# A decode block on one core: wq in five row loads, with the load of x between them on SyncE's queue

## The chip, the cores and the metric

The kernel runs on one core of one Trainium2 chip. The metric is device time in microseconds (us) for one execution.

## What is computed

One decode step of a transformer block for one token: a layernorm, attention over a long cache with 32 query heads and 4 key/value heads, a residual, a second layernorm and a gated feed-forward layer. Cut to what matters:

```python
# x (1,1,1024); k_cache, v_cache (1,4,65536,128); wq (1024,4096); wo (4096,1024)
# w_gate, w_up (1024,3584); w_down (3584,1024); all bfloat16
q = layernorm(x) @ wq                       # 32 heads of 128
p = softmax(q . k_cache * 128 ** -0.5)      # 8 heads share one k/v head
h = x + (p @ v_cache) @ wo
n = layernorm(h)
out = h + (gelu(n @ w_gate) * (n @ w_up)) @ w_down
```

Everything but x is read once: 8 MiB of wq, 64 MiB of keys, 64 MiB of values, 8 MiB of wo and three times 7 MiB of the feed-forward weights, 165 MiB (173.02 MB) in all.

## The kernel before, in words

**The ring.** All large tensors pass through one tile, `ring` (L86): 128 partitions, three slots of 64 KB per partition, so 8 MiB a slot. The helper `load` (L171 to L179) takes the next slot and issues one DMA on SyncE's queue. Each such DMA covers all 128 partitions, with one contiguous piece of DRAM per partition: 64 KB in a load of wq, keys, values or wo, 56 KB in one of w_gate or w_up.

**The order of the loads** on SyncE's queue is wq, then pieces of 8 MiB of keys and values in the order of `todo` (L389 to L392), then wo, w_gate, w_up, and w_down in five pieces of falling size (L591 to L611). A load waits, at its issue, until the work that read its slot's earlier content is done. The first three loads have three free slots; the fourth (the third of keys) needs wq's slot and so waits for the matmuls with wq.

**The start.** The function `first_load_leads` (L119) takes the first instruction of SyncE, the load of wq, out of the body of the program and puts it ahead of the barrier that all engines pass at the start. The load of x, 2 KB, into four rows (0, 32, 64, 96) of the tile `x_row` goes onto ScalarE's queue (L183) after VectorE has set `x_row` to zero (L182). Then:

- GpSimd and VectorE build constants (L187 to L203): the identities, `sel`, `hmask`, `esel`; GpSimd clears `wsel` (L198).
- When x has landed, VectorE transposes it (L230) and `layernorm_cols` (L207 to L226) runs a chain over VectorE, TensorE and GpSimd. Its result is put into the padded tile `xnz` (L234 to L238, L250).
- When wq has landed, 64 small matmuls (L254 to L257) form q in PSUM; VectorE transposes it (L260) and casts it (L261); four matmuls spread it over the partitions (L264), and ScalarE writes it into `wsel` (L268), the stationary operand of all score matmuls.
- The first key load is then transposed in place on VectorE (L287), scored on TensorE (L289 to L299), and so on through the key and value heads. TensorE's, VectorE's and ScalarE's orders in that part are written out by hand (`keep`, L134; the loop at L409).

The lines that matter here:

```python
wq_v = A_wq.rearrange("(p c) n -> p c n", c=DC)
nc.vector.memset(x_row[:], 0.0)
nc.scalar.dma_start(out=x_row[0:97:32, :], in_=A_x[0, 0].rearrange("(g n) -> g n", g=4))
assert DC * HD == 2 * CW
wq_t = load(wq_v[:])
```

Row p of the tile thus holds rows 8p to 8p+7 of wq, 64 KB that lie together in DRAM.

Of the kernel before, what the change touches and what calls it, by code (L numbers as in the profile page):

```python
# [17 lines left out]
def kernel(  # L18
# [13 lines left out]
    nc = tc.nc  # L32
    P = 128
    D = A_x.shape[-1]
    Hkv, Sk, Dh = A_k_cache.shape[1], A_k_cache.shape[2], A_k_cache.shape[3]
    HD = A_wq.shape[1]
# [10 lines left out]
    CW = 16384  # L47
# [29 lines left out]
    x_row = lead.tile([P, D // 4], BF16, name="x_row")  # L77
# [8 lines left out]
    ring = chpool.tile([P, NSLOT * 2 * CW], BF16, name="ring")  # L86
# [81 lines left out]
    slot = [NSLOT - 1]  # L168
    loads, pools, last = [], [], {}

    def load(src, off=0):  # L171
        n, w = src.shape[1], src.shape[2]
        if off == 0:
            slot[0] = (slot[0] + 1) % NSLOT
        assert off + n * w <= 2 * CW
        o = slot[0] * 2 * CW + off
        tv = ring[:, o:o + n * w].rearrange("p (n w) -> p n w", w=w)
        loads.append(nc.sync.dma_start(out=tv, in_=src).ins)
        return tv  # L179

    wq_v = A_wq.rearrange("(p c) n -> p c n", c=DC)
    nc.vector.memset(x_row[:], 0.0)  # L182
    nc.scalar.dma_start(out=x_row[0:97:32, :], in_=A_x[0, 0].rearrange("(g n) -> g n", g=4))  # L183
    assert DC * HD == 2 * CW
    wq_t = load(wq_v[:])

    make_identity(nc, ident_bf[:])  # L187
    make_identity(nc, ident_f[:])
# [11 lines left out]
    for bp in range(4):  # L200
        s0 = 64 * (bp // 2) + bp % 2
        nc.vector.tensor_copy(out=esel[:, bp, :, :],
                              in_=ident_bf[:, s0:s0 + 63:2].unsqueeze(1).to_broadcast([P, 4, 32]))  # L203
# [205 lines left out]
    for n, u in enumerate(units):  # L409
        what, g, li = u  # L410
# [237 lines left out]
```

## Time and profile before

| what | value |
|---|---|
| time, median of 3 runs | 407.19 us (407.12 to 407.48) |
| time of the profiled execution | 407.47 us |
| its span, first to last instruction | 405.7 us |
| read from HBM | 173.02 MB |
| busy: TensorE matmul, VectorE, ScalarE, GpSimd | 295.1, 204.1, 40.3, 7.5 us |
| DMA, mean over the span | 427 GB/s |
| issue to landing of an 8 MiB load of keys, of values (medians) | 38.4, 34.2 us |
| last matmuls that wait for a load start at | 401.7 us |

The profiled execution's own time is 0.07% above the median, and 1.8 us longer than its span; that is what lies around the span. The profile page lists busy times by engine, the span in 40 slices, the DMA queues, the chain of work that ended last, and the groups of instructions. The timeline lists instructions in order of time, with the start, the length, the engine, the line and the tiles; "<-" in brackets names what ended the wait before. SPq and ACTq are the queues of SyncE and ScalarE, where DMAs are issued; PEld is TensorE's loading of stationary operands.

### The profile page before, as it was taken

To read this page: it belongs to the slowest core of one execution; us is meant where nothing else is said; L and a number is where in the kernel's file an instruction comes from. 1 tells how busy PE (TensorE), PEld (TensorE's weight loads), DVE (VectorE), ACT (ScalarE), POOL (GpSimd) and SP (SyncE) were. 2 spreads that over 40 slices of the span, in tenths; PEclk is the share of its full clock that TensorE was granted. 3 is DMA by queue.
4 is the path that set the end of the run, shared out by engine and by line. 5 is a ranking of instruction groups with operands and counts; after the bars stand their busy time and mean duration, and the time that the engine had idled before them with its cause. 6 is when DMAs were issued, how large, how long until landed. Compare 5 with 4: busy or idle time off the path is not lost.

```text
span 405.7 us, 2613 instructions
## 1 busy us (share of the span) xinstructions
PE 295.1 (73%) x1519; PEld 59.5 (15%) x681; DVE 204.1 (50%) x187; ACT 40.3 (10%) x63; POOL 7.5 (2%) x17
## 2 busy tenths in 40 slices
PE   0150777657799696979969957997796899655286
PEld 0110111111111110131111103111110211211012
DVE  0210978999829743972596387609943100220211
ACT  1010000013000021100000312000022100100001
POOL 2000000000000000000000000000010000000000
PEclk9995589999899999769999968899899699886779
DMA  9999999999999999999999999999999999999996
GB/s 414 414 414 465 465 414 409 420 414 491 426 415 426 414 485 426 415 426 420 485 420 415 433 420 478 420 416 439 420 465 426 415 446 420 439 443 419 424 409 249
DMA packets 3629, 173.18 MB, mean 427 GB/s; under 512 B 414, under 2 KB 674, under 8 KB 802
## 3 DMA queue, kind: packets, MB, share of 16 engines
q1 hardware_dynamic: 3610, 173.02, 98.8%
q8 instruction: 8, 0.13, 0.1%
q14 instruction: 3, 0.02, 0.0%
q10 hardware_dynamic: 8, 0.00, 0.0%
HBM read 173.02 MB, written 0.00 MB: 426 GB/s over the span
## 4 chain that ended last, share of the span: by engine, by line
DMA 40%; PE 37%; DVE 19%; ACT 2%; issue 1%; ACTq 0%; DVEq 0%
DMA ring<-in_A_k_cache_dram 30%; PE acc_ps L157 16%; DVE ring L287 14%; DMA ring<-in_B_w_down_dram 11%; PE qk_ps L155 7%; PE qk_ps L157 6%; PE acc_ps L155 5%; DVE mx L312 2%; ACT sc L308 2%; DVE pT L345 1%; PE o_ps L155 1%; DVE acc_sb L368 1%; PE at_ps L155 1%; PE at_ps L157 0%; PE nb_ps L155 0%
## 5 line engine op out<-in xcount | busy, mean ns | idle before, releaser
L287 DVE STREAM_TRANSPOSE ring<-ring 128x2048 uint32<-128x2048 uint32 x64 | 142.5, 2279 | 37.4 <-DMA ring<-in_A_k_cache_dram 37.4
L155 PE MATMUL qk_ps<-ring,wsel 128*128 128x512 bf16 x256 | 107.7, 421 | 51.5 <-DVE ring L287 32.0
L157 PE MATMUL qk_ps<-ring,wsel 128*128 128x512 bf16 x256 | 107.1, 418 | 0.0
L157 PE MATMUL acc_ps<-ring,pT 128*128 128x512 bf16 x384 | 105.2, 383 | 0.0
L155 PEld LDWEIGHTS <-wsel 128*128 128x128 bf16 x256 | 27.2, 106 | 158.8 <-issue 143.2
L155 PE MATMUL acc_ps<-ring,pT 128*128 128x512 bf16 x128 | 49.2, 385 | 0.0
L312 DVE TENSOR_REDUCE mx<-qk_ps 128x1 f32<-128x1024 f32 x16 | 19.5, 1220 | 25.8 <-ACT sc L308 19.7
L345 DVE STREAM_TRANSPOSE pT<-pT 128x1024 bf16<-128x1024 bf16 x16 | 19.3, 1228 | 23.8 <-ACT pT L339 23.8
L308 ACT COPY sc<-qk_ps 128x1024 f32<-128x1024 f32 x12 | 12.1, 1012 | 151.0 <-PE qk_ps L157 151.0
L155 PEld LDWEIGHTS <-pT 128*128 128x128 bf16 x128 | 12.8, 100 | 90.8 <-issue 90.8
L368 DVE COPY acc_sb<-acc_ps 32x512 f32<-32x512 f32 x8 | 5.3, 666 | 29.5 <-PE acc_ps L157 29.5
L339 ACT ACTIVATE pT<-sc,nbias 128x1024 bf16<-128x1024 f32 x12 | 13.7, 1142 | 45.0 <-DVE nbias L331 42.1
L155 PE MATMUL wu_ps<-ring,hnz 128*32 128x448 bf16 x32 | 5.9, 738 | 8.8 <-DMA ring<-in_B_w_up_dram 8.8
L155 PE MATMUL ln_tot<-ln_s,ones_f 128*128 128x1 f32 x8 | 1.9, 311 | 13.5 <-DVE ln_s L209 11.7
L155 PE MATMUL wg_ps<-ring,hnz 128*32 128x448 bf16 x32 | 6.1, 737 | 6.8 <-DMA ring<-in_B_w_gate_dram 6.8
L155 PE MATMUL o_ps<-sel,acc_sb 128*128 128x8 f32 x32 | 6.6, 335 | 5.8 <-DVE rl L382 5.4
L155 PE MATMUL q_ps<-ring,xnz 128*32 128x512 bf16 x32 | 4.2, 502 | 9.0 <-DMA ring<-in_A_wq_dram 9.0
L370 ACT COPY acc_sb<-acc_ps 32x512 f32<-32x512 f32 x8 | 4.6, 578 | 58.7 <-DVE acc_sb L368 58.7
L511 DVE STREAM_TRANSPOSE wu_t<-wu_ps 128x448 f32<-128x448 f32 x2 | 1.2, 628 | 14.2 <-PE wu_ps L155 14.2
L511 DVE STREAM_TRANSPOSE wg_t<-wg_ps 128x448 f32<-128x448 f32 x2 | 1.2, 629 | 13.3 <-PE wg_ps L155 13.3
L260 DVE STREAM_TRANSPOSE q_t<-q_ps 128x512 f32<-128x512 f32 x2 | 1.3, 695 | 12.5 <-PE q_ps L157 12.5
L339 ACT ACTIVATE pT<-qk_ps,nbias 128x1024 bf16<-128x1024 f32 x4 | 4.5, 1114 | 29.8 <-PE acc_ps L157 16.8
(117 smaller groups left out, 98.5 us busy)
## 6 DMA issues: line engine op xcount, KB each, us to landing
ring<-in_B_w_gate_dram SPq DMA_DIRECT2D x1, 7168.0 KB, 35.2
ring<-in_B_w_up_dram SPq DMA_DIRECT2D x1, 7168.0 KB, 38.3
ring<-in_B_w_down_dram SPq DMA_DIRECT2D x1, 4096.0 KB, 39.2
ring<-in_B_w_down_dram SPq DMA_DIRECT2D x1, 2048.0 KB, 43.2
ring<-in_B_w_down_dram SPq DMA_DIRECT2D x1, 768.0 KB, 44.6
ring<-in_B_w_down_dram SPq DMA_DIRECT2D x2, 128.0 KB, 44.5
ring<-in_A_k_cache_dram SPq DMA_DIRECT2D x8, 38.4
ring<-in_A_v_cache_dram SPq DMA_DIRECT2D x8, 34.2
```

The costliest lines, as they stand in the source:

```text
L155: return pe(t.matmul(out, lhsT=lhsT, rhs=rhs, start=start, stop=stop, tile_position=tile_position, skip_group_check=skip_group_check))
L157: op = t.add_instruction(mybir.InstMatmult(name=nc.get_next_instruction_name(), engine=t.engine, start_tensor_calc=start, stop_tensor_calc ...
L260: nc.vector.transpose(out=q_t[:, k, :], in_=q_banks[k])
L287: dv(nc.vector.transpose(out=kt[:, c * w:(c + 1) * w], in_=kt[:, c * w:(c + 1) * w]))
L308: ac(nc.scalar.copy(out=sc[:], in_=flat))
L312: dv(nc.vector.tensor_reduce(out=state[("mx", g)][:, li:li + 1], in_=flat, axis=AX.X, op=ALU.max))
L339: ac(nc.scalar.activation(out=flat, in_=state.pop(("sc", g, li)), func=ACT.Exp, bias=st["nbias"][:, 0:1], scale=scale, accum_out=st["lpart ...
L345: dv(nc.vector.transpose(out=flat, in_=flat))
L368: dv(nc.vector.tensor_copy(out=acc_sb[sl, :], in_=acc[sl, c, :]))
L370: ac(nc.scalar.copy(out=acc_sb[sl, :], in_=acc[sl, c, :]))
L511: nc.vector.transpose(out=t[:, k, :], in_=banks[k][:, 0:HF * 32])
```

## The change

wq is no longer one load of 128 rows but five, of 16, 16, 32, 32 and 32 rows, all on SyncE's queue and into the same slot. The load of x moves from ScalarE's queue to SyncE's, between the second and the third of them. `first_load_leads` is unchanged and now takes the load of the first 16 rows ahead of the barrier.

```diff
 wq_v = A_wq.rearrange("(p c) n -> p c n", c=DC)
 nc.vector.memset(x_row[:], 0.0)
-nc.scalar.dma_start(out=x_row[0:97:32, :], in_=A_x[0, 0].rearrange("(g n) -> g n", g=4))
 assert DC * HD == 2 * CW
-wq_t = load(wq_v[:])
+slot[0] = 0
+wq_t = ring[:, 0:2 * CW].rearrange("p (n w) -> p n w", w=HD)
+
+def wq_rows(lo, hi):
+    loads.append(nc.sync.dma_start(out=wq_t[lo:hi], in_=wq_v[lo:hi]).ins)
+
+wq_rows(0, 16)
+wq_rows(16, 32)
+nc.sync.dma_start(out=x_row[0:97:32, :], in_=A_x[0, 0].rearrange("(g n) -> g n", g=4))
+for lo in range(32, P, 32):
+    wq_rows(lo, lo + 32)
```

The order of instructions changes with it in three places. On SyncE's queue stand: wq rows 0 to 15, the barrier, wq rows 16 to 31, x (which waits for the memset of `x_row`), the three loads of 32 rows, and then the keys as before. On VectorE the eight operations for `esel`, `sel` and `hmask` now stand ahead of the transpose of x; on GpSimd the memset of `xnz` stands ahead of the layernorm's power. On TensorE the order is the same; the first weight load from `xnz` and the first matmul with wq wait for the five loads where they waited for one.

## The prediction

> **What bounds the kernel now.** I read the page's slices first, then the issues of DMAs, then the timeline of the start and the chain of work that ended last. The slices and the sum of what was read:
>
> ```profile
> DMA  9999999999999999999999999999999999999996
> ...
> HBM read 173.02 MB, written 0.00 MB: 426 GB/s over the span
> ```
>
> The DMA row shows nine tenths or more in every slice but the last, while no engine comes near that over the span. From the timeline of the start, which names what each wait ended on:
>
> ```profile
> 0.00 0.38 SPq L178 DMA_DIRECT2D ring<-in_A_wq_dram  x1
> 9.75 0.62 DVE L230 STREAM_TRANSPOSE x_t<-x_row 128x256 bf16<-128x256 bf16 x1 [8.56 <-DMA x_row<-in_A_x_dram]
> 14.55 0.10 PEld L155 LDWEIGHTS <-xnz 128*32 128x32 bf16 x1 [1.72 <-DVE xnz L237]
> 21.89 0.62 PE L155 MATMUL q_ps<-ring,xnz 128*32 128x512 bf16 x4 [8.97 <-DMA ring<-in_A_wq_dram]
> 28.98 1.06 ACT L268 CAST wsel<-qr_ps 32x128 bf16<-32x128 f32 x4 [25.30 <-PE qr_ps L155]
> 41.17 11.09 DVE L287 STREAM_TRANSPOSE ring<-ring 128x2048 uint32<-128x2048 uint32 x5 [12.59 <-DMA ring<-in_A_k_cache_dram]
> ```
>
> wq is there at 21.89, the first keys at 41.17: 19.28 us for the next 8 MiB (8.389 MB), or 435 GB/s. Everything else in the start has room: xnz is ready at 14.55, 7.3 us before wq; wsel is done at 30.04, 11.1 us before the keys. The chain of work that ended last, farther on:
>
> ```profile
> 158.36 39.15 DMA ring<-in_A_k_cache_dram
> 197.53 8.90 DVE ring L287 x4
> ...
> 233.65 41.05 DMA ring<-in_A_k_cache_dram
> 274.73 8.90 DVE ring L287 x4
> ...
> 357.32 43.21 DMA ring<-in_B_w_down_dram
> ```
>
> Keys are there at 197.51 and at 274.70; between the two, four 8 MiB loads landed: 77.19 / 4 = 19.30 us each, the same pace. And a load takes about 39 us from issue to landing where 19.3 are its own: each is issued while the one ahead of it still has its whole time to go, so the stream never runs dry. It closes as a sum: 165 MiB at 19.29 us per 8 MiB is 397.9 us, plus 2.6 us (21.89 - 19.29) until the first load is at pace, is 400.5; the page's chain ends its last DMA at 357.32 + 43.21 = 400.53. The rest, to 405.7, is the tail behind the last rows of w_down. So **the one stream of loads sets the end**, and what an edit costs it anywhere is paid in full.
>
> **What the change removes.** One issue on ScalarE's queue (1.08 us, started at 1.07). Behind it there stood a table load that ended at 3.46, and ScalarE's next work is at 28.98: nothing gained.
>
> **What it moves.** x, on SyncE, waits for the memset of x_row, which ended at 1.04 (0.87 + 0.17). Behind it stand three loads of wq and then the keys, each an issue of 0.33 to 0.38 us, as the rows of SPq show. The last wq load is then issued by about 2.6 us and the keys by 3.3, instead of 0.78. What hides it: 2 MiB of wq are queued ahead of x, at least 2 x 2.41 = 4.8 us of stream from about 1.0 on, so to 5.8 us. Without that cover the stream would lose 0.35 us for each issue. x now lands behind 2 MiB: at some 7 us at today's pace, or after two loads at whatever pace they have. The chain from x to xnz took 14.55 - 9.75 = 4.8 us; the eight operations now ahead of it on VectorE (busy from 13.03 to 14.10 before) and the 0.31 us memset on GpSimd need only the identities (1.70 us) and run before x is there. xnz must be ready when wq is. Cost and gain: 0 as long as x lands 4.8 us before wq. The third key load waits for five semaphores of wq in place of one, but also, as before, for the matmuls with wq, which come later: 0.
>
> **What it adds: five loads with few rows each.** This is the disputed cost, and no row shows it: every large load of the trace spreads over 128 rows, its 16 DMA engines together at 435 GB/s (27.2 GB/s each). A load of 16 rows has 16 packets of 64 KB, one for each engine if they spread; but these engines all write into 16 neighbouring rows. *Lower end:* the engine is the limit and not the place it writes to. Then 8 MiB take 19.3 us in whatever pieces, and the cost is 0. *Upper end:* the rate goes with the rows. A row then takes 435 / 128 = 3.4 GB/s, 16 rows take 54 GB/s, and each of the five loads, whatever its height, lasts as long as a full one: 5 x 19.3 = 96.5 us, +77.2. In between, think of the store as having doors, each as fast as an engine, and ask how many of the 16 a load reaches. If 16 rows reach 2 doors (eight neighbouring rows to a door) and 32 rows 4, that is the upper end; with 4 and 8 doors each load lasts 4 x 2.41 = 9.65 us, 48.2 us for wq, +28.9; with 8 and 16 doors 4.83 each, 24.1 for wq, +4.8; with 16, nothing. What in the trace speaks for a limit on the store's side: the pace of 19.3 us is the same for wq, keys and values, early and late, under busy and idle engines, so it is a fixed one, and is reached with all rows in play. What speaks against it: engine and door would have to be equally fast. Of the four cases three cost. I take the value nearest the middle of the ends: the geometric mean of 19.3 and 96.5 is 43.2 us, and the case nearest to it is 4 and 8 doors, **48.2 us, +28.9**.
>
> [...]
>
> **The sum.** wq is there 28.9 us later, at 50.8. The keys follow in the queue at the old pace, and what lies between (8.15 us from wq to wsel, inside 19.28) shifts with both. No later place gives the time back, since the stream has no idle time to give. The profiled execution: 407.47 + 28.9 = 436.4; against the median, which lies 0.28 us lower, 407.19 + 28.9 = **436.1 us**. Own range of this case: 432 (some engines run ahead of others into the next load, and part of the waiting overlaps) to 442 (each of the four further loads also pays the 1.5 us that the first one takes beyond 19.3 us from its first packet at about 1.0).
>
> **The rivals.**
> - *Partial cost:* 8 and 16 doors, or doors shared so unevenly that the loads overlap: +4.8 to +24, 412 to 431 us. For it: queues of 16 engines need not march in step. Against: equal packets on equal engines, which now start within a us of each other (983 GB/s of packets start between 1.0 and 2.0 us, which is 15 of 64 KB).
> - *Rows are the limit:* +77.2, 484 us. Against: it takes the coarsest doors.
> - *The change does nothing,* because the rate belongs to the engine: 407.2 us, within 0.2%. For it: 27.2 GB/s on each of 16 engines, for any tensor.
> - *Faster, on the other side:* the place is the start of the stream. The first load needs 21.89 - 19.28 = 2.6 us beyond its pace, of which 1.0 us passes before nearly all first packets. The price is the 1.5 us left; if a load of 16 rows is set up sooner than one of 128, the most of it could go, say 1.1: 406.1 us. It decides only if 16-row loads run at the full 435 GB/s: already a pace 6% lower (1.1 of 19.3 us) on wq would eat it.
>
> **How the numbers follow.** Cases: +28.9 with its own range 0.70; partial cost 0.09; rows 0.05; nothing 0.09; faster 0.07. The bound of 0.2% (0.8 us) is about what a measurement of this kernel can tell from no change. Slower: 0.70 + 0.09 + 0.05 = 0.84; same 0.09; faster 0.07. The first two cases hold 0.79, so the range reaches down to the case of no change, the lower end of the unknown cost, at 406.4 (407.2 - 0.8), and holds 0.88; the upper end at 484 stays out. The likeliest case's own range is 432 to 442.
>
> **What would show it.** In the changed profile: the first matmul with wq at 50 to 52 us, not 21.89; the first key transpose 19.3 us behind it; in the slices of the first 48 us about 175 GB/s on average (8.39 MB in 48 us), first near 109, if a load of 1 MiB takes as long as one of 2; x transposed at about 21 us; later distances between landings still 19.3 us; all engines idle longer before their first keys. I am wrong if the first matmul with wq stays near 22 us, and partly wrong (the size of the doors) if it lies near 27 or 99. If wq lands late but the end does not move by as much, then the stream had idle time that I did not see.

## The result and the profile after

The changed kernel takes 436.68 us (median of 5 runs, 436.66 to 436.83) where the kernel before takes 407.48 (median of 5, 407.12 to 407.73): a ratio of 1.0721, 95% interval 1.0709 to 1.0733. It is 29.2 us slower. The span of its profiled execution (436.68 us) is 434.9 us, 29.2 more than before. The ratios below leave out runs that a slower state of the core disturbed; for the one kernel whose median that would shift, the profiled run is given instead.

The slices of the page after; the rows are the busy share of the DMA engines in tenths and the bytes moved:

```profile
DMA  9599999999999999999999999999999999999996
GB/s 193 97 193 193 289 398 470 398 466 404 465 404 464 405 458 410 458 410 454 416 452 416 448 422 446 422 446 423 440 429 446 428 436 434 426 418 454 431 405 262
...
HBM read 173.02 MB, written 0.00 MB: 398 GB/s over the span
```

The bytes are the same, and the engines are as busy as before in nearly all slices; but in the first four slices (43 us) they move less than half as much as later. A packet is counted whole in the slice in which it starts, so the 5 and the 97 of the second slice are no pause: most of that slice is filled by packets that started in the first. The engines are busy but not fast here: their packets last longer. The windows show how much longer. The first load of 16 rows is 16 packets of 64 KB, counted where they start, with the time that they took as a share of 16 engines over the window, here 1.0 to 3.0 us, of the changed kernel:

```profile
q1 hardware_dynamic: 16, 1.05, 427.5%
```

and the same window of the kernel before:

```profile
q1 hardware_dynamic: 15, 0.98, 145.5%
```

4.275 x 16 x 2.0 / 16 = 8.6 us for a packet, against 1.455 x 16 x 2.0 / 15 = 3.1. All 16 packets of the changed kernel start between 1.0 and 2.0 us, so all 16 engines work on the load of 16 rows at once; it is not that fewer engines serve a load of few rows. The timeline after, in the order of the lines shown of before:

```profile
0.00 1.11 SPq L188 DMA_DIRECT2D ring<-in_A_wq_dram  x2
...
1.87 1.39 SPq L188 DMA_DIRECT2D ring<-in_A_wq_dram  x3
...
3.30 54.25 SPq L178 DMA_DIRECT2D ring<-in_A_k_cache_dram  x3
...
21.00 0.63 DVE L239 STREAM_TRANSPOSE x_t<-x_row 128x256 bf16<-128x256 bf16 x1 [16.43 <-DMA x_row<-in_A_x_dram]
25.31 0.18 DVE L246 COPY xnz<-xn_bf 128x8 bf16<-128x8 bf16 x1
...
51.84 0.62 PE L155 MATMUL q_ps<-ring,xnz 128*32 128x512 bf16 x4 [27.67 <-DMA ring<-in_A_wq_dram]
...
59.16 1.06 ACT L277 CAST wsel<-qr_ps 32x128 bf16<-32x128 f32 x4 [56.87 <-PE qr_ps L155]
...
70.94 11.09 DVE L296 STREAM_TRANSPOSE ring<-ring 128x2048 uint32<-128x2048 uint32 x5 [12.17 <-DMA ring<-in_A_k_cache_dram]
```

wq is there at 51.84, 29.95 us later; the keys follow it by 19.10 us (19.28 before), so their pace is the old one; wsel is ready at 60.22, 10.7 us ahead of them. Farther on, the chain of work that ended last:

```profile
262.96 41.14 DMA ring<-in_A_k_cache_dram
304.12 8.90 DVE ring L296 x4
```

The same keys are there at 304.10, 29.40 later than at 274.70 before. So what wq lost at the start is carried to the end, nearly in full.

### The profile page after: what moved, and what is told of

The parts are those of the page before. It is cut to its first block, busy times and chain, and to the rows that moved or that the text cites. A ratio compares the mean times of both kernels' runs of the same rounds, so it can differ in the third digit from the quotient of the medians.

```text
span 434.9 us, 2618 instructions
## 1 busy us (share of the span) xinstructions
PE 297.6 (68%) x1516; PEld 59.3 (14%) x681; DVE 206.3 (47%) x187; ACT 40.3 (9%) x63; POOL 7.5 (2%) x17
## 4 chain that ended last, share of the span: by engine, by line
PE 47%; DMA 29%; DVE 17%; another core or an unknown queue 3%; ACT 2%; issue 1%; SPq 0%; ACTq 0%; DVEq 0%
PE acc_ps L157 17%; DVE ring L296 12%; DMA ring<-in_A_wq_dram 11%; DMA ring<-in_A_k_cache_dram 9%; PE qk_ps L155 9%; PE qk_ps L157 9%; DMA ring<-in_B_w_up_dram 9%; PE acc_ps L155 6%; DVE mx L321 2%; ACT sc L317 2%; DVE pT L354 2%; PE wu_ps L155 1%; PE wu_ps L157 1%; PE o_ps L155 1%
## 5 line engine op out<-in xcount | busy, mean ns | idle before, releaser
L155 PE MATMUL qk_ps<-ring,wsel 128*128 128x512 bf16 x256 | 108.7, 425 | 49.9 <-DVE ring L296 30.2
L157 PE MATMUL qk_ps<-ring,wsel 128*128 128x512 bf16 x256 | 108.3, 423 | 0.0
L155 PE MATMUL acc_ps<-ring,pT 128*128 128x512 bf16 x128 | 49.2, 385 | 0.0
```

Of the source, the lines that this page charges most:

```text
L155: return pe(t.matmul(out, lhsT=lhsT, rhs=rhs, start=start, stop=stop, tile_position=tile_position, skip_group_check=skip_group_check))
L157: op = t.add_instruction(mybir.InstMatmult(name=nc.get_next_instruction_name(), engine=t.engine, start_tensor_calc=start, stop_tensor_calc ...
```

## The experiments

The theory is a picture of the author's, an estimate: **doors**. Say that what a load writes to has 16 doors, each about as fast as one DMA engine (27.2 GB/s, a sixteenth of 435). In the changed kernel the packets of the two loads of 16 rows last from 1.0 to 19.8 us, 112 GB/s, which would be four doors; the second load of 32 rows runs at 206 GB/s, which would be about eight. That 64 neighbouring rows reach no more than eight is an assumption, and the halves try it. No trace shows a door; the runs show rates. The rivals: a price of each load; x on SyncE's queue; the reading side, where 16 engines now read DRAM that lies side by side; the number of rows in a load, whichever they are.

### The same five pieces by columns

```diff
-wq_rows(0, 16); wq_rows(16, 32); ...
+wq_cols(0, 1); wq_cols(1, 2)          # wq_t[:, lo:hi, :] <- wq_v[:, lo:hi, :]
 nc.sync.dma_start(out=x_row[0:97:32, :], ...)
+wq_cols(2, 4); wq_cols(4, 6); wq_cols(6, 8)
```

> Five loads in the same place and of the same bytes (1, 1, 2, 2, 2 MiB), x between the second and the third on SyncE as in the changed kernel, but each load is a column piece over all 128 rows. Doors (the rows that a load writes set its rate): all 16 doors in reach, wq there at about 22 us, 407.2 us, within 1. Rival, the cost is one of each load (four more loads cost 29.2 us, so 7.3 each, whatever rows they cover): 436. Rival, it is x on SyncE's queue: 436.

Measured: 407.40 us, ratio 0.9999 (0.9990 to 1.0008). The number of loads, their sizes and the place of x cost nothing. Its timeline:

```profile
7.26 0.63 DVE L239 STREAM_TRANSPOSE x_t<-x_row 128x256 bf16<-128x256 bf16 x1 [2.69 <-DMA x_row<-in_A_x_dram]
...
11.89 0.62 PE L155 MATMUL q_ps<-ring,xnz 128*32 128x512 bf16 x4 [1.47 <-DVE xnz L246]
...
41.18 11.08 DVE L296 STREAM_TRANSPOSE ring<-ring 128x2048 uint32<-128x2048 uint32 x5 [15.83 <-DMA ring<-in_A_k_cache_dram]
```

x comes 2.5 us earlier than before and the projection starts 10 us earlier, since each matmul waits only for its own columns: later ones wait until 17.02 and 21.88 us for theirs. Neither helps: the keys are there at 41.18, as before (41.17).

### x alone moved

```diff
-nc.scalar.dma_start(out=x_row[0:97:32, :], ...)
 wq_rows(0, P)
+nc.sync.dma_start(out=x_row[0:97:32, :], ...)
```

> wq in one load of 128 rows as before; only x moves, to SyncE's queue behind wq. Doors: the stream is as before, x lands behind 8 MiB at about 22 us instead of 9.75, xnz is ready 4.8 us later at about 27, q starts there and not at 21.9, wsel is done at about 35, still 6 us before the first keys at 41.2: 407.2 us, within 0.8. Rival, x on SyncE's queue costs: above 410.

Measured: 407.31 us, ratio 0.9999 (0.9990 to 1.0008). x lands at 21.9 and the projection starts at 26.55 instead of 21.89; the slack ahead of the keys takes it up: wsel is ready at 35.40, the keys are there at 41.07. x has no share in the cost.

### The row loads alone

The five loads of the change, with x left on ScalarE's queue (L183 as before).

> The five row loads of the changed kernel alone; x stays on ScalarE's queue as before. Doors: 436.5 us, wq there at about 51.8, as in the changed kernel. Rival, x between the loads has a share in the cost: below 435.

Measured: ratio 1.0717 (1.0696 to 1.0739); the profiled run took 436.61 us, with the first matmul of wq at 51.62. The whole cost is in the row loads.

### Halves

```diff
-wq_rows(0, 16); wq_rows(16, 32); ...
+wq_rows(0, 64); wq_rows(64, P)
```

> wq in two loads, rows 0 to 63 and 64 to 127; x on ScalarE's queue as before. Doors with eight of them shared by rows 0 to 63 and the other eight by rows 64 to 127: each load of 4 MiB runs at 8 doors, the pace of the 32-row loads of the changed kernel (2 MiB in 10.1 us), so 20.2 us each, wq there at about 43, 428 us. Rival, the rate goes with the number of rows (16 rows 109 GB/s, 32 rows 207, so 64 rows the full pace): 407. Rival, a price of each load: one more load, 414.5.

Measured: 428.32 us, ratio 1.0512 (1.0498 to 1.0527). Three windows follow: the kernel before and the halves, each from 2.6 us, where the kernel before reaches its pace (21.89 - 19.28), to the first matmul with wq, and between them the second 32-row load of the changed kernel. The last two columns are the busy share of the DMA engines and GB/s:

```profile
2.60:21.89 19.29, 1.18 (x5) 1.10 (x6) 3.12 (x18) 1.07 (x2) 1.70 (x3) 1.00 1.00 435
...
29.30:39.50 10.20, 0.00 (x0) 0.00 (x0) 0.00 (x0) 0.00 (x0) 0.00 (x0) 1.00 0.99 206
...
2.60:43.25 40.65, 1.18 (x5) 1.03 (x5) 3.11 (x18) 1.49 (x2) 2.13 (x3) 1.00 0.95 206
```

wq takes 40.65 us, 20.3 for each 64 rows, 206 GB/s: no more than 32 rows get. In the picture of doors, rows 32 to 63 would bring none that rows 0 to 31 do not have. The engines are busy for 0.95 of the time here too, so they are slow and not few.

### Far reads, near writes

```diff
-wq_rows(0, 16); wq_rows(16, 32); ...
+for j in range(4):
+    nc.sync.dma_start(out=wq_t[32 * j:32 * j + 32], in_=wq_v[j:P:4])
```

> Four loads of 32 neighbouring rows of the tile, each fed from every fourth 64 KB piece of wq in DRAM, so that the reads of a load lie 256 KB apart over all of wq and no longer side by side. (The tile's rows hold other rows of wq than x's entries belong to: the projection is not the reference's, its work is the same.) Doors (the writing side): 4 x 10.1 = 40.4 us for wq instead of 19.3, 428 us. Rival, the reading side (16 engines on neighbouring DRAM get in each other's way): 407. x is on ScalarE's queue as before.

Measured: 428.07 us, ratio 1.0505 (1.0488 to 1.0521), and in the window of its wq:

```profile
2.60:43.28 40.68, 1.17 (x5) 1.03 (x6) 3.12 (x18) 1.08 (x2) 1.70 (x3) 1.00 0.95 206
```

The same 206 GB/s, though the reads lie 256 KB apart. The reading side is not it.

### Near reads, far writes

```diff
+for j in range(4):
+    nc.sync.dma_start(out=wq_t[j:P:4], in_=wq_v[32 * j:32 * j + 32])
```

> The mirror of the kernel with reads far apart: four loads of 32 rows, read from 32 neighbouring pieces of wq (2 MiB that lie together), written into every fourth row of the tile. (Rows are permuted against x, so the projection is not the reference's; its work is the same.) The first key load waits for wq here too, 2.5 us. Doors, if the 32 rows reach all 16 and engines spread over them: 409.7. Doors with engines in step on half of them, or a rate by the number of rows: 40.4 us for wq and 430.8. Reading side: 430.8 too, but that is out already by its mirror.

Measured: 410.60 us, ratio 1.0081 (1.0064 to 1.0098). The timeline tells the pause from the pace:

```profile
22.66 0.62 PE L155 MATMUL q_ps<-ring,xnz 128*32 128x512 bf16 x4 [11.48 <-DMA ring<-in_A_wq_dram]
...
44.48 11.09 DVE L294 STREAM_TRANSPOSE ring<-ring 128x2048 uint32<-128x2048 uint32 x5 [14.30 <-DMA ring<-in_A_k_cache_dram]
```

wq is there at 22.66, 0.8 us later than in one load. Keys come 21.82 us behind it, 2.5 more than the usual 19.28, and are issued only at 22.60 (0.78 before): the pause that was foretold. Four loads of 32 rows run within 4% of the pace of one of 128, if their rows are spread; their packets last 2.4 us, as in the load of 128 rows, and 0.7 of the 0.8 us are lost by the end of the first 16 packets.

### Every second row

```diff
+for lo in range(2):
+    nc.sync.dma_start(out=wq_t[lo:P:2], in_=wq_v[lo:P:2])
```

> wq in two loads of 64 rows each, as many as in the halves, but every second row of the tile (and of wq), so that each load reaches over all 128 rows; x on ScalarE's queue. The dependency tracking makes the first key load wait here until wq has landed, so the stream pauses once, some 2.5 us (issue, first packet and slower first wave as at the start of the span). Doors, if engines spread over them at every moment: 409.7. Rival, the number of rows in a load sets its rate and not which rows: 428.3 + 2.5 = 430.8. Doors, with engines in step on eight of them at a time: also 430.8.

Measured: 410.26 us, ratio 1.0073 (1.0058 to 1.0088): wq at 22.23 (0.3 later), keys at 44.06 (2.5 us of pause; they are issued at 22.18). Loads of 64 rows cost 21.0 us as neighbours and little but the pause when spread. Their rates are 206 GB/s and 427 (8.389 MB from 2.6 to 22.23 us): here it is which rows a load writes that sets its rate, not how many.

### Sixteens

```diff
+for lo in range(0, P, 16):
+    wq_rows(lo, lo + 16)
```

> wq in eight loads of 16 neighbouring rows, x on ScalarE's queue. Doors: 16 rows reach four, each load lasts 9.3 to 9.65 us as the first two of the changed kernel, so 74.4 to 77.2 us for wq, +55.1 to +57.9: 462.4 to 465.2. Rival, the rate of a load goes otherwise with its height (16 rows held back in the changed kernel by the start alone, so 10.1 us for two of them as for one of 32): 428.

Measured: 462.15 us, ratio 1.1347 (1.1330 to 1.1364), 0.3 us below the range.

```profile
2.60:77.07 74.47, 1.17 (x4) 1.10 (x5) 3.12 (x18) 1.07 (x2) 1.70 (x3) 1.00 0.93 113
```

74.47 / 8 = 9.31 us for a load of 16 rows, 113 GB/s.

### The halves on two queues

```diff
 wq_rows(0, 64)
-wq_rows(64, P)
+nc.scalar.dma_start(out=wq_t[64:P], in_=wq_v[64:P])
```

> The two halves of 64 rows, but rows 64 to 127 are issued on ScalarE's queue (x behind them), so that loads to the two sets of eight doors are under way at the same time. Doors, if each engine takes turns between the queues and the engines stay in step: at each moment all are on one half, 206 GB/s, wq there at 43 and 428 us, as with both on one queue. Doors, if the engines get out of step or one engine has packets of both queues under way: all 16 doors are in use, wq there at 22, 407 us. A rate by the number of rows in a load, with nothing shared between loads of different queues: also 407.

Measured: 427.68 us (four runs, 427.42 to 431.72), ratio 1.0531 (1.0479 to 1.0582). The first keys were there at 61.67, 20.5 us late, as with both halves on one queue (62.32). The windows 5 to 8, 10 to 13, 15 to 18 and 20 to 23 us hold these packets (q1 is SyncE's queue, q10 ScalarE's):

```profile
q1 hardware_dynamic: 16, 1.05, 170.7%
...
q10 hardware_dynamic: 16, 1.05, 163.4%
...
q1 hardware_dynamic: 16, 1.05, 163.3%
...
q10 hardware_dynamic: 16, 1.05, 163.4%
```

All 16 engines take one packet of one queue, then all one of the other: 1.634 x 3.0 = 4.9 us for each packet, twice the 2.4 us of a load over all rows. In these windows the engines are in step. The rate is 216 GB/s from 2.6 to 22 us and 200 from 22 to 43, as with both halves on one queue (206): in the picture of doors, all engines would stand at the same eight at a time. Two queues do not win the loss back: 427.68 us against 428.32.

## Why the prediction was right

**The one stream sets the end: right.** The first matmul with wq came 29.95 us later, the first keys 29.77 and the end 29.2. That looks as if 0.75 us came back, but the packet records of the two traces show otherwise. The last packet of wq ends at 21.50 us before and at 50.80 after, 29.30 later; the last one of the first keys at 40.84 and 70.41, 29.57 later; the last one of w_down at 402.66 and 431.86, 29.20 later. So the stream lost 29.3 us on wq and kept that loss, within 0.3, to the end. The rest of the 29.95 lies between the last packet of wq and the first matmul: 0.39 us before, 1.04 after. It is 0.4 also for spread rows and for columns, and 0.9 to 1.3 for the other loads of neighbouring rows; why was not tried. The halves, the far reads and the sixteens repeat the rule: their last packets of wq end 20.8, 20.7 and 54.3 us late, and they take 21.0, 20.8 and 54.8 us more (medians against 407.3, 407.3 and 407.35).

**The value for the rows: right, by the middle case.** The sum took every load at 9.65 us, 48.2 for wq and 28.9 more than before, where the packets show 29.3 more: the term was 0.4 us too small. Measured alone, to the first matmul, 16 rows take 9.31 us and 2 MiB of 32 rows take 40.68 / 4 = 10.17, so the term was 0.3 too large for each load of 16 rows and 0.5 too small for each of 32: 2 x 9.31 + 3 x 10.17 = 49.1, where the changed kernel shows 51.84 - 2.61 = 49.2 in the same way of counting, the late matmul included. The forecast of 436.1 is 0.6 below the result: nearly all of it is that 0.4, and a median of before that was 0.3 lower in the runs shown first.

**The choice itself was less sure than the result makes it look.** From the rows of before alone, a geometric mean between two ends picked the case. That is no mechanism, and as far as those rows go the hit was luck. The result lies in that case's own range, 432 to 442; the range as a whole, from 406.4 up, would have held no change as well. The runs added rates that fit the case: 113 GB/s for 16 neighbouring rows, about four times 27.2; 206 for 32 and for 64, between seven and eight times; 418 (8.389 MB from 2.6 to 22.66 us) and 427 for every fourth and every second row, more than 15 times. That doors are the cause was not shown, and which rows hold each other back was tried only for these sets.

**The moves: right.** x was transposed at 21.00 us (21 foretold), its result ready at 25.5, 26 us ahead of wq; the last wq issue ended at 3.26, later than the 2.6 foretold, and the keys were issued from 3.30. The stream had packets all the while: those of the first two loads lasted until 19.8. Two readings of before were a little off, and nothing hung on them. ScalarE's next work behind the table load is an exponential at 3.48, not the cast at 28.98. And the sum of the stream closed at 400.5 by luck: at 400.53 only the 2 MiB piece of w_down had landed, and the packets of the smaller pieces behind it end at 402.66.

**The rivals.** That the cost is none fell with the result. Partial cost fell with the measured rates (113 GB/s for 16 rows and 206 for 32, where 8 and 16 doors would give 218 and 435), and because the engines stay in step; the two queues show this best (16 packets of one queue, then 16 of the other). The upper end, a rate by rows, fell with the sixteens: 113 GB/s and not 54. The faster start has no support either: the small first loads by columns leave the keys at 41.18, and the spread rows, at 427 and 418 GB/s, had wq at 22.2 and 22.7, not below 21.9.

## What to carry to other kernels

Where one stream of loads sets the end, cut a load by columns and not by rows: five column pieces cost nothing here, five row pieces 29 us. If rows must be cut, take every second or fourth row (wq 0.3 and 0.8 us later here), and see that dependency tracking doesn't turn that into a pause (2.5 us here). In a profile, read GB/s and the time of a packet beside the busy share of the DMA engines: they were nine tenths busy at a quarter to a half of their pace.

## What was not expected of the hardware

- Read as doors, which is an estimate, 206 GB/s over eight are 25.8 a door, 113 over four 28.2, and 435 over sixteen 27.2. The order is odd. The 206 is the same whether reads are near (the halves) or far; for 16 rows that was not tried, nor was the cause.
- A small load was held up by loads on the other queue, and longer with a large one ahead of it on its own: VectorE starts on x, 2 KB and alone on ScalarE's queue, at 9.75 us before and at 17.67 with both halves on SyncE's queue, and behind a half of wq on ScalarE's queue only at 49.28. That made wsel, ready at 62.1, later than the first keys (61.67).
